# Attention and a gated MLP on one core: q loaded by rows of nine tokens, output stores in one DMA each, and new instruction lists

## The chip, the cores and the metric

The kernel runs on one core of a Trainium2 chip. The core has five engines, each with an instruction stream of its own: TensorE (PE) multiplies matrices, VectorE (DVE), ScalarE (ACT) and GpSimd (POOL) work on tiles, and SyncE (SP) here issues nearly all the transfers. Transfers between HBM and the core's SBUF run on 16 DMA engines, which all of them share. The engines meet through semaphores.

The metric is the device time of one execution in microseconds (us). Before the change the median of three runs is 245.94 us, from 245.34 to 246.67. A separate execution was recorded by the hardware profiler.

## The reference

There are 8 batches of 8 heads, 576 tokens of 64 values a head, and 32 packing queries `p` a head. Two softmax attentions follow each other, and then an MLP with a gated activation over all 4608 tokens:

```python
def _attn_ref(q, k, v, p):
    scale = 1.0 / np.sqrt(q.shape[-1])
    def sm_attn(qq, kk, vv):
        s = scale * np.matmul(qq, kk.transpose(0, 1, 3, 2))
        s = s - np.max(s, axis=-1, keepdims=True)
        a = np.exp(s)
        a = a / (np.sum(a, axis=-1, keepdims=True) + 1e-09)
        return np.matmul(a, vv)
    p_packed = sm_attn(p, k, v)
    return sm_attn(q, p_packed, p_packed)

def _moe_ref(x, w_in, w_out, beta):      # x: (4608, 512), heads side by side
    h = x @ w_in                         # (4608, 2048)
    g = h * (1.0 / (1.0 + np.exp(-beta * h)))
    return g @ w_out                     # (4608, 512)
```

All inputs and the output are float32.

## The kernel before

The work goes batch by batch, and several batches are under way at once. For each batch `b`:

- `plan_loads` loads k, q and v as float32 and casts them to bf16. For batches 0 and 1 (`PE_BATCHES = 2`) a partition takes nine tokens of a head in a row (`quarter`, L460: packets of 9 x 64 x 4 = 2304 bytes, two DMAs of 576 KB for each of k, q, v), the casts go to whichever engine the lists name, and TensorE transposes. For batches 2 to 7 there is one DMA of 1 MB (`main`, L444: a partition takes four tokens of a head, packets of 1 KB) for the first 512 tokens (`SM`), and two of 64 KB (`rest`, L452: 256-byte packets) for the last 64 (`SR`). GpSimd casts them in three pieces (`piece`, L476, and `tail`, L487). The float32 buffer of each of k, q, v exists once, so a load waits for the casts of the batch before; the bf16 buffer exists once too, so a cast waits for the last reader of the batch before.
- `transpose_dma` (L558) has k and q of batches 2 to 7 transposed by a DMA, issued on SP (task `("tr", b, x, 0)`).
- `plan_attention` computes scores `s1`, exponentials `e1`, sums `z1` and the packed values `pun`/`pp`; then the second attention: scores `s2` (L778, which needs the transposed q), `e2`, sums `z2`, and the normalised weights `A2`. Instead of forming the attention's output, it multiplies the packed values with `w_in` (`w`, giving `W`).
- `plan_mlp` has 16 blocks `h` (`W` times `A2`, activated by ACT into `g`) for the first 512 tokens, and `hr`/`gr` for the last 64. The product with `w_out` is made in plain form for batch 0 (tasks `o`), and for the others by seven products instead of eight (`plan_seven`, L1135: sums `S` on DVE, products `p`/`P` 1 to 7, results read by copies and additions `R11` to `R22+`).
- The result of a batch stands in two tiles `o_sb` of 512 KB, of which the pool holds two (`OUTS`). So `R11` of a batch waits until the first store of the batch before has landed, and `R22` until the second has; product 6 waits for `R11`, product 3 for `R22`. Each tile is stored by task `("store", n)`, where batch `b` has n = 2b and 2b + 1. For batches 0 and 1 a store is two DMAs of 256 KB in packets of 2 KB (L1028, L1189), for the others one DMA of 512 KB in packets of 4 KB (L1193). The last 64 tokens of two batches are stored together as `("store", b, 4)`.
- `plan_small` loads beta and p. The p rows of batches 0 and 1 come in two DMAs of 64 KB (`load_first`, L1283), those of all batches in one of 512 KB (`load_p`, L1287).

The order on each engine is fixed in advance: `SEQUENCE` (L62) lists every task by engine. `Planner.run` walks through these lists, and emits the instructions. It also puts small matmuls of ones (`keep_warm`, 128x128, written `o_ps<-ones` in the profile) into TensorE's stream where its estimate of the times leaves TensorE without work, up to 60 us. They compute nothing that is used, and once they are in the stream, TensorE runs them. The lists hold, for SP, the loads, the transposes, and the stores; SP waits at each for its conditions, and what is listed behind it waits too.

Of the kernel before, what the change touches and what calls it, by code (L numbers as in the profile page):

```python
# [8 lines left out]
B, H, S, D = 8, 8, 576, 64  # L9
# [12 lines left out]
NC = 4  # L22
# [24 lines left out]
PE_BATCHES = 2  # L47
HALVED = (0,)
def TILED(key):
# [14 lines left out]
        ("tr", 0, "k", 0), ("brow", 0), ("p0_tr", 0), ("bcol",), ("tr", 0, "k", 1), ("trr", 0, "k"), ("brow", 1),  # L64
        ("tr", 0, "q", 0), ("s1r", 0), ("s1", 0, 1), ("s1", 0, 0), ("tr", 0, "q", 1), ("p0_tr", 1), ("trr", 0, "q"),
        ("z1", 0), ("brow", 2), ("pun", 0, 0), ("pun", 0), ("tr", 1, "k", 0), ("s2", 0, 0), ("tr", 1, "k", 1),
        ("z2", 0, 0), ("s2", 0, 1), ("z2", 0, 1), ("w", 0, 0), ("tr", 1, "q", 0), ("trr", 1, "k"), ("z2", 0, 2),
        ("s1r", 1), ("s1", 1, 0), ("s1", 1, 1), ("w", 0, 1), ("h", 0, 1), ("h", 0, 0), ("h", 0, 3), ("h", 0, 7),
        ("tr", 1, "q", 1), ("h", 0, 2), ("h", 0, 6), ("z1", 1), ("o", 0, 2, 1), ("h", 0, 4), ("pun", 1, 0),
        ("pun", 1), ("brow", 3), ("h", 0, 5), ("o", 0, 3, 1), ("o", 0, 3, 3), ("o", 0, 2, 3), ("o", 0, 2, 5),  # L70
        ("s2", 1, 0), ("o", 0, 2, 7), ("o", 0, 3, 5), ("o", 0, 3, 7), ("z2", 1, 0), ("w", 0, 2), ("z2", 1, 1),
        ("o", 0, 0, 1), ("o", 0, 0, 3), ("w", 1, 0), ("o", 0, 1, 1), ("h", 0, 11), ("h", 0, 8), ("w", 0, 3),
        ("o", 0, 0, 5), ("o", 0, 0, 7), ("trr", 1, "q"), ("h", 0, 10), ("h", 0, 9), ("o", 0, 1, 3), ("w", 1, 1),
        ("h", 0, 14), ("h", 0, 13), ("w", 1, 2), ("h", 0, 15), ("h", 1, 6), ("w", 1, 3), ("h", 0, 12), ("o", 0, 1, 5),
        ("o", 0, 1, 7), ("h", 1, 1), ("h", 1, 11), ("p_tr", 0), ("h", 1, 4), ("h", 1, 8), ("p_tr", 1), ("o", 0, 0, 9),
        ("o", 0, 1, 9), ("h", 1, 2), ("o", 0, 0, 11), ("h", 1, 12), ("o", 0, 0, 13), ("h", 1, 9), ("o", 0, 0, 15),
        ("s2", 1, 1), ("h", 1, 10), ("h", 1, 0), ("o", 0, 1, 11), ("o", 0, 1, 13), ("o", 0, 1, 15), ("s1r", 2),
        ("s1", 2, 0), ("o", 0, 2, 9), ("h", 1, 5), ("h", 1, 14), ("s1", 2, 1), ("o", 0, 2, 11), ("o", 0, 3, 9),
        ("o", 0, 2, 13), ("o", 0, 2, 15), ("o", 0, 3, 11), ("z1", 2), ("o", 0, 3, 13), ("h", 1, 3), ("h", 1, 13),
        ("o", 0, 3, 15), ("h", 1, 15), ("h", 1, 7), ("p", 1, 1, 0), ("pun", 2, 0), ("z2", 1, 2), ("pun", 2),  # L80
        ("p", 1, 1, 1), ("p", 1, 1, 2), ("P", 1, 1), ("s2", 2, 0), ("s2", 2, 1), ("p", 1, 2, 0), ("hr", 0, 0),
        ("p", 1, 2, 1), ("p", 1, 2, 2), ("z2", 2, 0), ("P", 1, 2), ("hr", 0, 1), ("w", 2, 0), ("p", 1, 6, 0),
        ("p", 1, 6, 1), ("p", 1, 6, 2), ("P", 1, 6), ("p", 1, 5, 0), ("p", 1, 5, 1), ("p", 1, 5, 2), ("z2", 2, 1),
        ("hr", 1, 0), ("P", 1, 5), ("p", 1, 7, 0), ("s1r", 3), ("p", 1, 7, 1), ("s1", 3, 0), ("p", 1, 7, 2),
        ("s1", 3, 1), ("P", 1, 7), ("z2", 2, 2), ("p", 1, 3, 0), ("p", 1, 3, 1), ("p", 1, 3, 2), ("w", 2, 2),
        ("h", 2, 6), ("p", 1, 4, 0), ("p", 1, 4, 1), ("h", 2, 2), ("h", 2, 1), ("p", 1, 4, 2), ("z1", 3), ("h", 2, 8),
        ("h", 2, 9), ("P", 1, 4), ("pun", 3, 0), ("pun", 3), ("h", 2, 11), ("hr", 1, 1), ("o", 1, 4, 1), ("w", 3, 0),
        ("h", 2, 3), ("h", 2, 12), ("o", 1, 4, 3), ("P", 1, 3), ("h", 2, 13), ("h", 2, 7), ("o", 1, 4, 5),
        ("o", 1, 4, 7), ("h", 2, 0), ("h", 2, 15), ("o", 1, 4, 9), ("w", 3, 2), ("h", 2, 14), ("h", 2, 4),
        ("o", 1, 4, 11), ("o", 1, 4, 13), ("h", 2, 5), ("h", 2, 10), ("o", 1, 4, 15), ("p", 2, 1, 0), ("s2", 3, 0),  # L90
        ("s2", 3, 1), ("p", 2, 1, 1), ("p", 2, 1, 2), ("P", 2, 1), ("p", 2, 2, 0), ("p", 2, 2, 1), ("z2", 3, 0),
        ("p", 2, 2, 2), ("z2", 3, 1), ("p", 2, 6, 0), ("p", 2, 6, 1), ("p", 2, 6, 2), ("z2", 3, 2), ("P", 2, 6),
        ("P", 2, 2), ("s1r", 4), ("s1", 4, 1), ("s1", 4, 0), ("hr", 2, 0), ("p", 2, 7, 0), ("p", 2, 7, 1),
        ("p", 2, 5, 0), ("p", 2, 5, 1), ("p", 2, 7, 2), ("p", 2, 5, 2), ("P", 2, 5), ("h", 3, 8), ("h", 3, 12),
        ("z1", 4), ("pun", 4, 0), ("h", 3, 13), ("hr", 2, 1), ("pun", 4), ("P", 2, 7), ("p", 2, 3, 0), ("h", 3, 10),
        ("h", 3, 9), ("w", 4, 0), ("h", 3, 3), ("h", 3, 1), ("p", 2, 3, 1), ("h", 3, 2), ("p", 2, 3, 2), ("h", 3, 11),
        ("P", 2, 3), ("h", 3, 15), ("w", 4, 2), ("h", 3, 5), ("h", 3, 6), ("p", 2, 4, 0), ("p", 2, 4, 1), ("h", 3, 0),
        ("h", 3, 7), ("p", 2, 4, 2), ("P", 2, 4), ("h", 3, 4), ("h", 3, 14), ("s2", 4, 0), ("s2", 4, 1),
        ("p", 3, 1, 0), ("p", 3, 1, 1), ("p", 3, 1, 2), ("P", 3, 1), ("p", 3, 2, 0), ("p", 3, 2, 1), ("p", 3, 2, 2),
        ("z2", 4, 0), ("P", 3, 2), ("z2", 4, 1), ("p", 3, 6, 0), ("p", 3, 6, 1), ("p", 3, 6, 2), ("P", 3, 6),  # L100
        ("s1r", 5), ("s1", 5, 1), ("z2", 4, 2), ("s1", 5, 0), ("p", 3, 5, 0), ("p", 3, 5, 1), ("p", 3, 5, 2),
        ("p", 3, 7, 0), ("hr", 3, 0), ("P", 3, 5), ("p", 3, 7, 1), ("p", 3, 7, 2), ("h", 4, 6), ("z1", 5),
        ("h", 4, 13), ("P", 3, 7), ("hr", 3, 1), ("pun", 5, 0), ("h", 4, 1), ("p", 3, 3, 0), ("pun", 5), ("h", 4, 12),
        ("p", 3, 3, 1), ("h", 4, 14), ("p", 3, 3, 2), ("h", 4, 15), ("w", 5, 0), ("h", 4, 4), ("h", 4, 9),
        ("p", 3, 4, 0), ("p", 3, 4, 1), ("h", 4, 2), ("h", 4, 8), ("P", 3, 3), ("p", 3, 4, 2), ("h", 4, 0),
        ("h", 4, 7), ("P", 3, 4), ("w", 5, 2), ("h", 4, 3), ("h", 4, 10), ("o", 3, 4, 1), ("o", 3, 4, 3), ("h", 4, 5),
        ("h", 4, 11), ("o", 3, 4, 5), ("o", 3, 4, 7), ("o", 3, 4, 9), ("s2", 5, 0), ("s2", 5, 1), ("p", 4, 1, 0),
        ("o", 3, 4, 11), ("p", 4, 1, 1), ("z2", 5, 0), ("p", 4, 1, 2), ("P", 4, 1), ("z2", 5, 1), ("z2", 5, 2),
        ("o", 3, 4, 13), ("o", 3, 4, 15), ("p", 4, 6, 0), ("p", 4, 6, 1), ("hr", 4, 0), ("hr", 4, 1), ("p", 4, 2, 0),
        ("p", 4, 2, 1), ("p", 4, 2, 2), ("P", 4, 2), ("h", 5, 15), ("h", 5, 1), ("p", 4, 6, 2), ("P", 4, 6),  # L110
        ("h", 5, 3), ("h", 5, 10), ("s1r", 6), ("s1", 6, 0), ("p", 4, 5, 0), ("p", 4, 7, 0), ("p", 4, 5, 1),
        ("p", 4, 5, 2), ("s1", 6, 1), ("h", 5, 7), ("P", 4, 5), ("h", 5, 13), ("p", 4, 7, 1), ("p", 4, 7, 2),
        ("z1", 6), ("pun", 6, 0), ("P", 4, 7), ("p", 4, 3, 0), ("h", 5, 4), ("pun", 6), ("h", 5, 8), ("p", 4, 4, 0),
        ("p", 4, 3, 1), ("h", 5, 6), ("h", 5, 9), ("w", 6, 0), ("h", 5, 11), ("p", 4, 4, 1), ("h", 5, 0),
        ("p", 4, 3, 2), ("h", 5, 14), ("P", 4, 3), ("h", 5, 5), ("p", 4, 4, 2), ("h", 5, 2), ("P", 4, 4),
        ("h", 5, 12), ("s2", 6, 0), ("s2", 6, 1), ("hr", 5, 0), ("p", 5, 1, 0), ("p", 5, 1, 1), ("p", 5, 1, 2),
        ("P", 5, 1), ("p", 5, 2, 0), ("p", 5, 2, 1), ("z2", 6, 0), ("p", 5, 2, 2), ("z2", 6, 1), ("P", 5, 2),
        ("p", 5, 6, 0), ("p", 5, 6, 1), ("p", 5, 6, 2), ("P", 5, 6), ("s1r", 7), ("s1", 7, 1), ("p", 5, 5, 0),
        ("s1", 7, 0), ("z2", 6, 2), ("p", 5, 5, 1), ("p", 5, 5, 2), ("hr", 5, 1), ("P", 5, 5), ("p", 5, 7, 0),
        ("w", 6, 2), ("p", 5, 7, 1), ("p", 5, 7, 2), ("P", 5, 7), ("h", 6, 5), ("p", 5, 3, 0), ("p", 5, 3, 1),  # L120
        ("h", 6, 3), ("h", 6, 10), ("p", 5, 3, 2), ("p", 5, 4, 0), ("h", 6, 4), ("z1", 7), ("h", 6, 9), ("pun", 7, 0),
        ("pun", 7), ("h", 6, 0), ("P", 5, 3), ("h", 6, 2), ("p", 5, 4, 1), ("h", 6, 1), ("p", 5, 4, 2), ("h", 6, 15),
# [241 lines left out]
class Kernel:  # L364
# [65 lines left out]
    def plan_loads(self, b):  # L430
        nc = self.nc
        rank = 100 * b
        early = b < PE_BATCHES
        for xi, x in enumerate("kqv" if b == 0 else "kvq"):
            src = self.src[x]
            last = [] if b == 0 else [("cast", b - 1, x, i) for i in range(2)]
            lastr = [] if b == 0 else [("cast", b - 1, x, 2)]

            def opened(x=x, b=b):
# [1054 lines left out]
```

## Time and profile before

| | us |
|---|---|
| median of three runs | 245.94 |
| lowest and highest | 245.34, 246.67 |
| profiled execution: time | 247.44 |
| profiled execution: span, first to last instruction | 245.7 |
| TensorE busy in the span | 235.1 |
| ScalarE busy | 175.0 |
| VectorE busy | 157.6 |
| GpSimd busy | 54.8 |

The profiled execution is 1.5 us above the median. Its span leaves out 1.7 us around the first and the last instruction. Times in the profile count from the start of the span.

A busy share alone says little here: TensorE's stream contains the fillers, and matmuls overlap, with ends that are modelled. What TensorE needs for a task is read from the start of its first matmul to the start of the next task's. In lines of the timeline the columns are start, duration, engine and source line, operation, what is written and read, shape, count, and in brackets the idle time before it with what ended it. `SPq` is the issuing side of SyncE; the duration of a DMA there is the time that issuing it held SyncE, not its transfer.

The page also gives the mean granted TensorE clock, 0.993, and the DMA queue that SP uses: 67,504 packets and 53.75 MB, 80.3% of the 16 engines' time over the span.

### The profile page before, as it was taken

Reading aid. Unit: us, or ns where it says so; the run is one execution under the profiler, and the core shown is the slowest. Engines: PE = TensorE matmul, PEld = TensorE weight load, DVE = VectorE, ACT = ScalarE, POOL = GpSimd, SP = SyncE. Lnnn points to the kernel's source line nnn. Section 1 sums busy time; section 2 is a strip of 40 time slices with the busy share of each in tenths; the row PEclk is TensorE's granted clock in tenths of the full one; section 3 lists DMA queues with packets and bytes.
Section 4 is the critical chain, followed back from the end, with each engine's and each line's share of the span. In section 5 each row is a group of like instructions: output and inputs, shape, how many; then the busy total and the mean of one; then the engine's idle time right before and its main releaser. Section 6 shows DMA issues by size and latency. Waiting matters only on the chain.

```text
span 245.7 us, 6197 instructions
## 1 busy us (share of the span) xinstructions
PE 235.1 (96%) x2619; PEld 160.8 (65%) x2619; DVE 157.6 (64%) x259; ACT 175.0 (71%) x310; POOL 54.8 (22%) x73
## 2 busy tenths in 40 slices
PE   7999999999899998999899997899999999999993
PEld 7787743355578644884588554776687737668893
DVE  3858979996878668656875654544768157813821
ACT  4157879889779767876788679287787769868320
POOL 3211006424500726013503251060005100000000
PEclk9999999999999999999999999799999999999999
DMA  7999999999999998997899999969491640004124
GB/s 234 382 388 399 400 385 348 374 216 279 226 209 270 331 226 188 198 325 193 184 236 290 259 179 345 240 199 182 143 278 27 99 165 9 0 4 173 43 85 129
DMA packets 67699, 54.27 MB, mean 221 GB/s; under 512 B 39508, under 2 KB 59220, under 8 KB 67160
## 3 DMA queue, kind: packets, MB, share of 16 engines
q1 hardware_dynamic: 67504, 53.75, 80.3%
q8 instruction: 20, 0.33, 0.6%
q10 hardware_dynamic: 168, 0.14, 0.2%
q14 instruction: 7, 0.06, 0.1%
HBM read 37.36 MB, written 9.44 MB: 191 GB/s over the span
## 4 chain that ended last, share of the span: by engine, by line
PE 62%; DMA 19%; SPq 9%; DVE 3%; POOL 3%; ACT 2%; issue 1%; POOLq 0%; DVEq 0%
PE o_ps L395 34%; PE h_ps L395 15%; DMA k<-in_k_dram 8%; SPq L455 3%; DMA out_dram<-o_sb 3%; SPq L560 3%; DMA v<-in_v_dram 3%; DMA vr<-in_v_dram 2%; PE w_ps L395 2%; DMA qT<-q_bf 2%; PE s_ps L395 2%; PE hr_ps L395 2%; PE brow_ps L395 2%; DMA x<-in_moe_beta_dram 1%; SPq L1028 1%
## 5 line engine op out<-in xcount | busy, mean ns | idle before, releaser
L945 ACT ACTIVATE g_main<-h_ps 128x512 bf16<-128x512 f32 x128 | 72.0, 596 | 34.4 <-PE h_ps L395 34.1
L395 PEld LDWEIGHTS <-g_main 128*128 128x128 bf16 x624 | 59.5, 99 | 23.5 <-issue 2.4
L395 PE MATMUL h_ps<-A2T,W_bf 128*128 128x512 bf16 x256 | 69.7, 379 | 0.1
L395 PE MATMUL o_ps<-w_out_bf,g_main 128*128 128x256 bf16 (+1 forms) x400 | 61.8, 293 | 0.0
L910 DVE SCALAR_TENSOR_TENSOR W_bf<-w_ps,rz,beta_bc 128x512 bf16<-128x512 f32 x64 | 44.7, 744 | 16.6 <-PE w_ps L395 16.3
L395 PEld LDWEIGHTS <-W_bf 128*128 128x128 bf16 x512 | 33.1, 100 | 21.5 <-issue 6.3
L410 ACT ACT_TABLE_LOAD x24 | 30.8, 1283 | 1.1 <-PEq L1478 0.7
L395 PE MATMUL o_ps<-w_sum,g_main 128*128 128x256 bf16 x224 | 30.8, 273 | 0.0
L395 PE MATMUL o_ps<-w_sum,g_sum 128*128 128x256 bf16 x224 | 28.6, 273 | 2.2 <-DVE o_sb L1183 2.2
L1181 DVE TENSOR_TENSOR o_sb<-o_ps,o_sb 128x512 f32<-128x512 f32 x21 | 14.5, 689 | 21.4 <-PE o_ps L395 14.3
L395 PEld LDWEIGHTS <-g_sum 128*128 128x128 bf16 x224 | 21.3, 98 | 7.1 <-issue 2.5
L482 POOL CAST q_bf<-q 128x1024 bf16<-128x1024 f32 x12 | 13.0, 1093 | 57.2 <-DMA q<-in_q_dram 57.2
L1183 DVE COPY o_sb<-o_ps 128x512 f32<-128x512 f32 x16 | 11.0, 689 | 13.4 <-PE o_ps L395 9.3
L395 PE MATMUL o_ps<-ones 128*128 128x128 bf16 x219 | 17.5, 235 | 1.1 <-DVE ones L1246 1.1
L482 POOL CAST v_bf<-v 128x1024 bf16<-128x1024 f32 x12 | 12.4, 1047 | 23.9 <-DMA v<-in_v_dram 16.7
L482 POOL CAST k_bf<-k 128x1024 bf16<-128x1024 f32 x12 | 12.5, 1050 | 22.1 <-DMA kT<-k_bf 9.4
L395 PEld LDWEIGHTS <-ones 128*128 128x128 bf16 x219 | 14.9, 107 | 3.3 <-issue 1.6
L395 PE MATMUL o_ps<-w_out_bf,g_rem 128*128 128x512 bf16 (+1 forms) x80 | 16.5, 336 | 0.0
L965 ACT ACTIVATE g_rem<-hr_ps 128x512 bf16<-128x512 f32 x16 | 9.3, 596 | 7.6 <-PE hr_ps L395 7.6
L1151 DVE TENSOR_TENSOR g_sum<-g_main 128x2048 bf16<-128x2048 bf16 x7 | 9.0, 1279 | 6.9 <-ACT g_main L945 6.9
L810 ACT ACTIVATE E2T<-s_ps,rz 128x512 bf16<-128x512 f32 x16 | 10.6, 685 | 3.7 <-PE s_ps L395 2.0
L395 PEld LDWEIGHTS <-pp 64*32 64x32 bf16 x368 | 3.9, 89 | 12.9 <-issue 7.6
(111 smaller groups left out, 264.5 us busy)
## 6 DMA issues: line engine op xcount, KB each, us to landing
k<-in_k_dram SPq DMA_DIRECT2D x6, 1024.0 KB, 11.0
q<-in_q_dram SPq DMA_DIRECT2D x6, 1024.0 KB, 7.7
v<-in_v_dram SPq DMA_DIRECT2D x6, 1024.0 KB, 8.1
out_dram<-o_sb SPq DMA_DIRECT2D x10, 512.0 KB, 3.1
w_in<-in_moe_w_in_dram SPq DMA_DIRECT2D x4, 1024.0 KB, 10.3
w_out<-in_moe_w_out_dram SPq DMA_DIRECT2D x4, 1024.0 KB, 11.8
out_dram<-o_sb SPq DMA_DIRECT2D x12, 256.0 KB, 3.6
k<-in_k_dram SPq DMA_DIRECT2D x4, 576.0 KB, 6.4
```

The lines of the kernel that those rows point to most:

```text
L395: return self.nc.tensor.matmul(out, lhsT, rhs, start=start, stop=stop, tile_position=pos, skip_group_check=True)
L410: self.nc.scalar.preload_act_table_set(SETS[mode])
L455: nc.sync.dma_start(t[64 * g : 64 * g + 64, :].rearrange("p (h d) -> p h d", h=4), src[b, 4 * g : 4 * g + 4, SM:S, :].rearrange("h p d -> ...
L482: self.copy[engine](o[:, 0:2048].rearrange("p (t h d) -> p h t d", t=4, h=8)[:, h], t[:, 0:2048].rearrange("p (h t d) -> p h t d", h=8, t= ...
L560: nc.sync.dma_start_transpose(t[:], st[b, x][:])
L810: nc.scalar.activation(st[b, "E2"][:, i, 0:SM], st[b, "s2", i][:], AF.Exp, scale=st[b, "rz1"][:, 2 + i : 3 + i])
L910: nc.vector.scalar_tensor_tensor(st[b, "W"][:, r, cols].rearrange("q (f p) -> q f p", f=4), st[b, "w", m][:].rearrange("q (p f) -> q f p", ...
L945: nc.scalar.activation(st[b, "g"][:, ft, :], st[b, "h", ft][:], AF.Silu)
L965: nc.scalar.activation(st[b // 2, "gr"][:, 8 * half : 8 * half + 8, o : o + 64], st[b, "hr", half][:].rearrange("p (f n) -> p f n", f=8), ...
L1151: nc.vector.tensor_tensor(o, x, y, op)
L1181: nc.vector.tensor_tensor(o, x, o, ALU.add)
L1183: self.copy[engine](o, x)
```

## The change

Four things are changed together.

1. **q of batches 2 to 6** (`BY_ROWS`) is loaded with nine tokens of a head in each partition, as in the early batches: four DMAs of 288 KB with packets of 2304 bytes (`pairs`). GpSimd casts it in two halves, each of four instructions, which also order the tokens in such a way that a partition of the output tile holds two neighbouring rows of the output. The scores `s2` read the transposed q by this order. q of batch 7, and all k and v, stay as they were, except that the last 64 tokens now stand in the same float32 buffer as the others, so that the next batch's load waits for all three casts.
2. **Stores**: with the tokens in this order the two tiles of batches 0 to 6 are each stored by one DMA with packets of 4 KB (`self.rows`). For batches 0 and 1 this replaces two DMAs of 2 KB packets; their q is transposed in another order for it.
3. **p**: the rows of batches 0 and 1 come in one DMA of 128 KB, and are cast, transposed (four matmuls) and placed together; the other load has only batches 2 to 7.
4. **The lists** of all five engines are replaced. Tasks move along their list, and some change their engine.

```diff
+BY_ROWS = range(2, 7)
...
+            def pairs(i, x=x, b=b, src=src, opened=opened):
+                t = opened() if i == 0 else self.t[b, x, "32"]
+                for e in range(2):
+                    nc.sync.dma_start(
+                        t[:].rearrange("p (i e f) -> p i e f", i=2, e=2)[:, i, e],
+                        src[b].rearrange("(a i e) (s t) d -> i e a s (t d)", e=2, i=2, t=TS)[i, e],
+                    )
...
+                if rows:
+                    for e in range(2):
+                        o = self.t[b, x][:, h].rearrange("p (t e d) -> p e t d", t=TS, e=2)[:, e]
+                        n = self.t[b, x, "32"][:, h].rearrange("p (e t d) -> p e t d", t=TS, e=2)[:, e]
+                        self.copy[engine](
+                            o[:, 0:8].rearrange("p (r m e) d -> p r e m d", r=2, m=2),
+                            n[:, 0:8].rearrange("p (r e m) d -> p r e m d", r=2, m=2),
+                        )
+                        self.copy[engine](o[:, 8], n[:, 8])
+                    return
...
+                    if b in BY_ROWS:
+                        q = q[h, TS * (c % 2) : TS * (c % 2) + TS, g : g + 64]
+                        q = q[:, 8] if rest else q[:, 0:8]
...
-                if b < PE_BATCHES:
-                    rows = self.out[S * b : S * b + S, :].rearrange("(s t) n -> s t n", t=TS)
-                    for e in range(2):
-                        nc.sync.dma_start(rows[:, 2 * t - 2 + e : 2 * t + 1 + e : 2], o[64 * e : 64 * e + 64])
+                if b < PE_BATCHES or b in BY_ROWS:
+                    nc.sync.dma_start(self.rows(b, t // 2), o[:])
                     return
...
+    def rows(self, b, i):
+        rows = self.out[S * b : S * b + S, :].rearrange("(s t) n -> s t n", t=TS)[:, 4 * i : 4 * i + 4]
+        return rows.rearrange("s (e m) n -> e s (m n)", e=2)
...
-        def load_first(b):
-            self.p0[b] = t = self.sm.tile([128, 2, D], f32, tag="E2T", name="p0")
-            nc.sync.dma_start(t[:], self.p[b].rearrange("(e x) s d -> (x s) e d", e=2))
+        def load_first():
+            self.p0 = t = self.sm.tile([128, 4 * D], f32, tag="E2T", name="p0")
+            nc.sync.dma_start(t[:], self.p[0:PE_BATCHES].rearrange("b h (x t) d -> (b h x) (t d)", t=4))
```

The list of SP from the first q by rows to the last load of batch 6, before and after:

```diff
-        ("ld", 2, "q", 0), ("tr", 2, "k", 0), ("ld", 2, "q", 2), ("ld", 2, "v", 0), ("ld", 2, "v", 2),
-        ("ld", 3, "k", 0), ("ld", 3, "k", 2), ("tr", 2, "q", 0), ("store", 0), ("store", 1), ("tr", 3, "k", 0),
-        ("ld", 3, "v", 0), ("ld", 3, "v", 2), ("ld", 3, "q", 0), ("ld", 4, "k", 0), ("ld", 3, "q", 2),
-        ("ld", 4, "v", 0), ("ld", 4, "k", 2), ("ld", 4, "v", 2), ("tr", 3, "q", 0), ("store", 2), ("tr", 4, "k", 0),
-        ("store", 3), ("ld", 4, "q", 0), ("ld", 5, "k", 0), ("ld", 5, "k", 2), ("ld", 4, "q", 2), ("ld", 5, "v", 0),
-        ("tr", 4, "q", 0), ("store", 4), ("tr", 5, "k", 0), ("store", 5), ("ld", 5, "q", 0), ("ld", 5, "q", 2),
-        ("ld", 5, "v", 2), ("ld", 6, "k", 0), ("ld", 6, "k", 2), ("ld", 6, "v", 0), ("ld", 6, "v", 2),
-        ("tr", 5, "q", 0), ("ld", 6, "q", 0), ("store", 1, 4), ("store", 7), ("store", 6), ("ld", 7, "k", 0),
+        ("ld", 2, "q", 0), ("ld", 2, "q", 1), ("tr", 2, "k", 0), ("ld", 2, "v", 0), ("ld", 2, "v", 2),
+        ("ld", 3, "k", 0), ("ld", 3, "k", 2), ("tr", 2, "q", 0), ("store", 0), ("ld", 3, "v", 0), ("tr", 3, "k", 0),
+        ("store", 1), ("ld", 3, "v", 2), ("ld", 3, "q", 0), ("ld", 3, "q", 1), ("ld", 4, "k", 0), ("ld", 4, "v", 0),
+        ("ld", 4, "v", 2), ("ld", 4, "k", 2), ("ld", 4, "q", 0), ("tr", 3, "q", 0), ("store", 2), ("tr", 4, "k", 0),
+        ("ld", 4, "q", 1), ("store", 3), ("ld", 5, "v", 0), ("store", 1, 4), ("ld", 5, "k", 0), ("ld", 5, "q", 0),
+        ("ld", 5, "k", 2), ("tr", 4, "q", 0), ("ld", 5, "q", 1), ("ld", 6, "k", 0), ("store", 4), ("tr", 5, "k", 0),
+        ("store", 5), ("ld", 5, "v", 2), ("tr", 5, "q", 0), ("ld", 6, "q", 0), ("ld", 6, "v", 0), ("ld", 6, "k", 2),
+        ("ld", 6, "v", 2), ("ld", 6, "q", 1), ("store", 7), ("store", 6), ("ld", 7, "k", 0),
```

At the start of the lists, the casts, transposes and copies of the first two batches are dealt out among ACT, DVE and POOL in another way. For example, ACT now casts the second half of k of batch 1 before the exponentials `e2` of batch 0, and DVE casts a half of the second `w_in` block between `A2` 0 of batch 0 and `W` 0 of batch 0.

## Prediction

> **What bounds the kernel now.** I read the page first (busy shares and the 40 slices), then TensorE's timeline, the list of waits, the busy times by stage, and SyncE's queue.
>
> ```profile
> span 245.7 us, 6197 instructions
> ...
> PE 235.1 (96%) x2619; PEld 160.8 (65%) x2619; DVE 157.6 (64%) x259; ACT 175.0 (71%) x310; POOL 54.8 (22%) x73
> ...
> PEclk9999999999999999999999999799999999999999
> DMA  7999999999999998997899999969491640004124
> ```
>
> TensorE is issuing nearly all the time, and the DMA engines are full for the first 60% of the span. So there are two questions: what of TensorE's time is no work, and which transfer it waits for. The timeline of TensorE answers the first (start, duration, shape and count; in brackets the idle time before it and what ended it):
>
> ```profile
> 17.58 1.17 PE L395 MATMUL o_ps<-ones 128*128 128x128 bf16 x18
> ...
> 23.41 1.61 PE L395 MATMUL o_ps<-ones 128*128 128x128 bf16 x26
> ...
> 67.90 0.41 PE L395 MATMUL s_ps<-qT,pp 64*32 64x512 bf16 x8 [0.99 <-DMA qT<-q_bf]
> ...
> 97.12 0.41 PE L395 MATMUL s_ps<-qT,pp 64*32 64x512 bf16 x8 [0.71 <-DMA qT<-q_bf]
> ...
> 121.74 0.41 PE L395 MATMUL s_ps<-qT,pp 64*32 64x512 bf16 x8 [1.22 <-DMA qT<-q_bf]
> ...
> 154.24 1.03 PE L395 MATMUL o_ps<-w_sum,g_sum 128*128 128x256 bf16 x8 [2.23 <-DVE o_sb L1183]
> ...
> 156.76 2.80 PE L395 MATMUL o_ps<-w_out_bf,g_main 128*128 128x256 bf16 x16
> ...
> 177.18 2.79 PE L395 MATMUL o_ps<-w_out_bf,g_main 128*128 128x256 bf16 x24
> ```
>
> Ends are modelled, so I count from start to start. The `ones` matmuls are fillers, 0.056 us each (eighteen from 17.58 to 18.67, less 0.09 for a change of tile shape). From the first `h` at 27.11 on, real work follows back to back, except in four places: before `s2` of batches 2, 3 and 4, which wait for the transposed q, and at 152 us. Start to start these cost 1.06, 0.78 and 1.29, and 2.3 us. After the last one TensorE is slow: 16 matmuls of 256 columns take 2.64 us (to 159.40), where 24 take 2.62 at 177.18, so these 16 lose 0.9, and the `hr` before them 0.7. The stage view has the granted clock of that stretch (PE, PEld, DVE, ACT, POOL busy, clock, DMA share, GB/s):
>
> ```profile
> 150.00:160.00 10.00, 7.77 (x74) 5.93 (x72) 4.03 (x6) 5.26 (x9) 1.04 (x1) 0.83 1.05 280
> ```
>
> What held 152 us is in the waits (us, times, longest) and in SyncE's queue:
>
> ```profile
> DVE o_sb L1183 <- DMA out_dram<-o_sb: 4.1, 2, 3.6
> ```
>
> ```profile
> 140.12 3.40 SPq L560 DMA_TRANSPOSE qT<-q_bf  x1
> 143.57 0.58 SPq L447 DMA_DIRECT2D q<-in_q_dram  x1
> 144.20 1.22 SPq L1038 DMA_DIRECT2D out_dram<-o_rest  x2
> 145.52 1.34 SPq L1193 DMA_DIRECT2D out_dram<-o_sb  x2
> 146.96 0.45 SPq L447 DMA_DIRECT2D k<-in_k_dram  x1
> 147.51 10.00 SPq L560 DMA_TRANSPOSE kT<-k_bf  x1
> ```
>
> The stores of batch 3 stand behind a 1 MB load, so the copy that reuses their buffer waits. A transpose holds SyncE until what was queued before it has landed: this k transpose for 10.00 us, until 157.51; the loaded k landed at 157.43. After 160 us the DMA share falls below 1, and TensorE has no gaps over 0.3 us. The avoidable time is 1.06 + 0.78 + 1.29 + 2.3 + 1.6 = 7.0 us, plus what part of the 219 fillers (12.4 us) earlier data would remove.
>
> **The change, part by part.**
>
> *The start.* The changed program has 189 fillers, 30 fewer: 30 x 0.056 = -1.7 us. Two more p transposes cost +0.1; 16 transposes of 96 columns in place of 128 give -0.2. That is -1.8 if data comes in time. The DMA share is 1.04 to 1.08 from 4 us on, so I walked the landings: the one p load is 128 packets of 1 KB in place of 512 of 256 B, which by the packet times in the trace (46 and 18 ns, 16 engines) is 0.37 for 0.58 us, so the loads of batch 1 come about 0.4 us earlier. In the new order `s2` of batch 0 can start near 16.3 (18.67 before). The gain shrinks at ACT, where the cast of k (1.15 us) now stands ahead of the first exp, and at VectorE, where a weight cast of the second `w_in` stands ahead of `W` 0: landing 22.0, cast 0.7, reciprocal 0.25, then `W` 0.75, q cast 0.75, `W` 0.75, `A2` 0.68, so first `h` at 26.5, not 27.1. With the 12 fewer fillers after it (0.7): **-1.2**, bounds 0 and -1.8.
>
> *q by rows, batches 2 to 6.* Before, 1024 packets of 1 KB and 512 of 256 B a batch; after, 512 of 2304 B. The nearest rows are the early q and v loads (576 KB in the same packets), which land 1.5 us apart; I take 1.6 each for later crowding, 3.2 a batch. A 1 MB load takes 3.5 (landings between 76.7 and 92.6 are 3.1 to 4.7 us apart) and a pair of 64 KB 0.6: 4.1. So -0.9 a batch, bounds 0 and -1.1. [...]
> GpSimd's casts become 2 x (512 + 64) elements for each half. Rows of 1.04 us for 1024 and 0.40 for 256 give 0.62 and 0.24: 1.7 a half, 3.4 a batch for 2.5. GpSimd is 22% busy and the transposes wait for the queue anyway: nothing; uncovered it would be +0.9 a batch. `s2` reads 64 columns at a time for 128, the same 512: nothing, bounds 0 and +0.1 a batch.
>
> *Stores of batches 0 and 1 as one DMA of 4 KB packets.* Before, two stores took 5.1 us of the queue (67.6 to 72.7), 2.5 each; a 512 KB store in 4 KB packets and the k transpose behind it took 4.6 us (121.7 to 126.3), less 3.0 for a transpose (64.6 to 67.6): 1.6. I take 1.8, so 4 x -0.7 = -2.8 us, bounds 0 and -3.6.
>
> *The queue's new order*, where gain and loss lie. I walk it from the k transpose of batch 2 (landing 54.5, now 53.7: the two p loads and q are 0.8 shorter). It runs at 1.06 of the sum of these prices: from there to 126.3 the old order sums to 67.8 and took 71.8. Due times are TensorE's durations by kind (`h` or `o` 0.43 a pair, `p` 0.44, `hr` 0.47, `w` 0.56, `s1` 0.23, `s2` 0.37) summed in the new order from the first `h` at 26.5, with the new waits as they come.
> - q of batch 2: v, k, transpose, 11.4 x 1.06 = 12.1, lands 65.8 (67.6 before); `s2` is due about 66.6. Gap gone.
> - Store 1 now stands behind the v load of batch 3 and a k transpose: 1.8 + 3.5 + 3.2 + 1.8, x 1.06, lands 76.7. The copy of quarter 22 of batch 1 needs its buffer, and product 3 behind it is due at 76.2: 76.7 + 0.7 copy + 0.3 gives 77.7, **+1.4**, bounds 0 and +2.5 (store as dear as before, 0.7, and queue at 1.10). Behind that copy VectorE holds `A2` of batch 2, not due for 1.5 us.
> - q of batches 3 and 4: land near 94.5 and 117, due near 95.9 and 118. Both gaps gone.
> - k of batch 5: its transpose now has q of batch 5 (3.2), k of batch 6 (3.5) and a small store (0.7) ahead that stood behind it before. Old landing 126.3, less 0.8, less 0.9 x 2 q batches and 0.9 on q of batch 4, less 2.8, plus 7.4: 127.4. `s1` of batch 5 is due near 125.4: **+2.0**, bounds 0 and +6. Store 4 stands just ahead, lands near 124, and holds quarter 11 of batch 3, due 121.9, by 1 us of the same 2.
> - Stores 7 and 6: q of batch 5 lands 133, five loads behind it end near 142, store 7 lands near 144 and 6 near 147; needed at 149. The 2.3 us gap and the slow clock behind it go: -3.9.
> - From 150 on the transposes land 2 us and more ahead of their use. The tail of 3.7 us after TensorE's last matmul has the same stores: nothing.
>
> Sum: -1.2 - 7.0 + 1.4 + 2.0 + 0.6 for smaller waits like the three of 0.2 to 0.3 us in the trace of before = **-4.2 us**. That is made on the profiled execution (span 245.7, time 247.4, so span 241.5, time 243.2). It lies 1.5 above the runs' median, 245.94, from which -4.2 gives **241.7 us**. Half a per cent, 1.2 us, is about what a measurement of this kernel can tell from no change.
>
> **The rivals.**
> - *The new waits don't come* (queue at 1.00 of the prices): -1.8 - 7.0 + 0.3 = -8.5, 237.4 us. For: the early stage's 1.5 us spacing. Against: 71.8 for 67.8. Chance 0.12.
> - *The waits only move:* both new waits at the upper middle of their bounds, +2.2 and +4.2 with 1.6 of slow clock, as after the 2.2 us idle: -1.2 - 7.0 + 8.0 = -0.2, 245.7 us (with 0.6 of small waits, 246.3). For: the stretch from 54.5 to 76.7 ran at 1.10. Chance 0.16.
> - *Slower: k of batch 5 decides.* Loads of batches 5 and 6 now run ahead of its transpose. If the queue runs at 1.15, it lands at 53.7 + 69.7 x 1.15 = 133.9 (69.7 is the new sum), 8.5 us late, plus 1.6 of clock: -1.2 - 7.0 + 1.4 + 10.1 = +3.3, 249.2 us. It decides from a landing past 130.5. For: 72 us of full queue lie ahead of it and nothing can overtake. Against: no stretch above 1.10. The same comes if rows and 4 KB packets save nothing (the change not doing what it says): +0.9 x 3 + 2.8 = 5.5 later. Chance 0.14.
> - My forecast, 0.58, with its own range 239.5 to 244.0.
>
> **The numbers.** Faster: 0.58 x 0.98, 0.12, and a quarter of the second rival's 0.16: 0.73. Same: the rest of that case and a little of the forecast: 0.13. Slower: 0.14. The range leaves out half of the first rival and most of the third: 238.5 to 246.5.
>
> **What would show it.** Right: `s2` of batches 2 to 4 without idle time on the q transposes; no gap near 152 and a clock of 1.00 there; 576 KB q loads at 3.2 us of queue a batch; gaps of 1 to 2 us at 76 (behind a store) and at 125 (behind kT). Wrong: first `h` not before 27.1; kT of batch 5 landing past 130; a stall over 2 us with the clock below 0.9 behind it; or gaps on VectorE or ACT work, which the trace of before doesn't have after 27 us and the new lists could bring.

## The result and the profile after

| | before | after |
|---|---|---|
| median, us | 245.97 | 440.44 |
| lowest and highest, us | 245.34, 246.67 | 440.14, 441.58 |
| ratio, 95% interval | | 1.791 (1.786 to 1.797) |
| span of the profiled execution, us | 245.7 | 438.3 |
| mean granted TensorE clock | 0.993 | 0.800 |

Here and below, ratios and their intervals leave out executions that took over 1.5% longer than the fastest of the same kernel, and medians count all.

The forecast was 241.7 us, in a range of 238.5 to 246.5. The kernel became 79% slower. The page of the changed kernel, first the busy times, then three rows of the 40 slices, then the chain of work that ended last:

```profile
span 438.3 us, 6166 instructions
...
PE 267.9 (61%) x2591; PEld 173.6 (40%) x2591; DVE 155.2 (35%) x251; ACT 179.5 (41%) x316; POOL 63.8 (15%) x100
...
PE   8999920937592033908170469702398459979386
...
PEclk9999975788698557976875588955889598969869
DMA  8999694973145993424949395214899390110113
...
DMA 37%; SPq 33%; PE 23%; DVE 2%; issue 2%; ACT 1%; POOL 1%; ACTq 0%; DVEq 0%; POOLq 0%
```

VectorE and ScalarE are busy for about as long as before (155.2 and 179.5 us against 157.6 and 175.0), and GpSimd for 9.0 us more (63.8 against 54.8): their work does not explain 194 us. TensorE stands idle in whole slices, the DMA row is low at the same time, and the chain of waits is made of transfers (37%) and of SyncE standing at its issues (33%). So the machine waits for transfers while the transfer engines look idle. The waits name them (us, times, longest):

```profile
POOL q_bf L509 <- DMA q<-in_q_dram: 102.7, 16, 19.3
...
DVE o_sb L1215 <- DMA out_dram<-o_sb: 61.9, 5, 23.1
ACT o_sb L1215 <- DMA out_dram<-o_sb: 61.8, 6, 22.8
```

These are the two transfers that the change rewrote: q by rows, and the stores of rows. VectorE's copies into a reused output tile waited 4.1 us for stores before. The first place is at 40 us, in SyncE's queue and in the stages (in the second view: PE, PEld, DVE, ACT, POOL busy, clock, DMA share, GB/s):

```profile
40.64 17.73 SPq L470 DMA_DIRECT2D q<-in_q_dram  x4
58.48 15.22 SPq L585 DMA_TRANSPOSE kT<-k_bf  x1
```

```profile
52.00:58.00 6.00, 5.91 (x35) 2.39 (x32) 5.91 (x11) 5.46 (x10) 0.85 (x2) 1.00 0.13 50
58.00:64.00 6.00, 0.00 (x0) 0.00 (x0) 1.74 (x2) 0.71 (x3) 0.79 (x2) 0.77 0.13 50
```

From 52 to 64 us only q loads of batch 2 move. The DMA share is 0.13, which is 2/16, and the rate 50 GB/s, for 359 to 400 between 10 and 50 us of the kernel before. So, by the share, two engines of 16 carry them and 14 stand still. In the trace's packet records, exactly two packets are under way for some 151 us of the changed kernel, for 3 or 4 us of the kernel before. The median packet is as long as before (95 ns for 2304 bytes in both; 160 ns before and 159 after for 4096). By that, a load of 288 KB takes 128 x 95 / 2 = 6.1 us, and a store of 512 KB 128 x 159 / 2 = 10.2 us; from first to last packet the trace has 5.9 to 7.7 us and 10.0 to 11.9. There are 20 such loads and 14 such stores: 122 + 143 us on two engines.

What the two transfers share is the shape of their HBM side: `[2, 64, 576]` for a load and `[2, 64, 1024]` for a store. The outermost count is 2. Every large load and store of the kernel before has 64 or more there.

That the count of 2 holds the DMA share at 2/16 is a guess up to here; the experiments test it.

Behind the waits, the clock: where TensorE has nothing to do it falls to 0.77 (58 to 64 us) and to 0.50 (64 to 70 us). It does not cause the idle time: in 52 to 58 us the clock is 1.00 and the share already 0.13.

### The profile page after: what moved, and what is told of

Its sections match the earlier page's. It is cut to its first block, busy times and chain, and to the rows that moved or that the text cites. A ratio compares the mean times of both kernels' runs of the same rounds, so it can differ in the third digit from the quotient of the medians.

```text
span 438.3 us, 6166 instructions
## 1 busy us (share of the span) xinstructions
PE 267.9 (61%) x2591; PEld 173.6 (40%) x2591; DVE 155.2 (35%) x251; ACT 179.5 (41%) x316; POOL 63.8 (15%) x100
## 4 chain that ended last, share of the span: by engine, by line
DMA 37%; SPq 33%; PE 23%; DVE 2%; issue 2%; ACT 1%; POOL 1%; ACTq 0%; DVEq 0%; POOLq 0%
DMA out_dram<-o_sb 23%; SPq L585 16%; PE o_ps L394 12%; SPq L470 9%; PE h_ps L394 7%; DMA kT<-k_bf 5%; SPq L447 3%; DMA v<-in_v_dram 3%; SPq L455 3%; DMA qT<-q_bf 2%; DMA k<-in_k_dram 2%; SPq L1219 2%; DMA w_in<-in_moe_w_in_dram 1%; PE w_ps L394 1%; PE s_ps L394 1%
## 5 line engine op out<-in xcount | busy, mean ns | idle before, releaser
L394 PE MATMUL o_ps<-w_sum,g_sum 128*128 128x256 bf16 x224 | 42.3, 353 | 74.0 <-ACT o_sb L1215 49.4
L394 PEld LDWEIGHTS <-g_main 128*128 128x128 bf16 x624 | 64.0, 105 | 52.2 <-issue 28.0
L394 PE MATMUL o_ps<-w_out_bf,g_main 128*128 128x256 bf16 (+1 forms) x400 | 70.4, 320 | 21.1 <-DVE o_sb L1215 20.0
L394 PE MATMUL h_ps<-A2T,W_bf 128*128 128x512 bf16 x256 | 76.2, 401 | 5.4 <-DVE A2T L881 5.4
L394 PEld LDWEIGHTS <-g_sum 128*128 128x128 bf16 x224 | 27.0, 125 | 86.9 <-issue 78.6
L1215 ACT COPY o_sb<-o_ps 128x512 f32<-128x512 f32 x13 | 7.6, 586 | 66.4 <-DMA out_dram<-o_sb 61.8
L509 POOL CAST q_bf<-q 128x512 bf16<-128x512 f32 x20 | 13.2, 662 | 115.8 <-DMA q<-in_q_dram 102.7
L394 PE MATMUL s_ps<-qT,pp 64*32 64x512 bf16 x56 | 3.7, 449 | 34.9 <-DMA qT<-q_bf 34.9
L394 PEld LDWEIGHTS <-kT 128*128 128x128 bf16 (+1 forms) x180 | 8.2, 117 | 27.1 <-DMA kT<-k_bf 25.5
L394 PE MATMUL s1r_ps<-pT,kT 128*128 128x128 bf16 (+1 forms) x20 | 2.8, 259 | 24.6 <-DMA kT<-k_bf 24.6
```

The costliest lines, as they stand in the source:

```text
L394: return self.nc.tensor.matmul(out, lhsT, rhs, start=start, stop=stop, tile_position=pos, skip_group_check=True)
L509: self.copy[engine](o[:, 0:8].rearrange("p (r m e) d -> p r e m d", r=2, m=2), n[:, 0:8].rearrange("p (r e m) d -> p r e m d", r=2, m=2),)
L1215: self.copy[engine](o, x)
```

## The experiments

Each was executed at least once, with a profile; where an interval is given, there are 6 or 12 executions, beside 11 to 23 of the kernel before. Theory: a transfer runs on as many engines as its outermost count allows. The rivals: the new lists or GpSimd's casts of q by rows are at fault, or only one of the two transfers is.

**Loads on 16 engines, stores as changed.**

```diff
-                for e in range(2):
+                for a in range(2):
                     nc.sync.dma_start(
-                        t[:].rearrange("p (i e f) -> p i e f", i=2, e=2)[:, i, e],
-                        src[b].rearrange("(a i e) (s t) d -> i e a s (t d)", e=2, i=2, t=TS)[i, e],
+                        t[64 * a : 64 * a + 64].rearrange("p (i e f) -> p i e f", i=2, e=2)[:, i],
+                        src[b].rearrange("(a i e) (s t) d -> i a s e (t d)", e=2, i=2, t=TS)[i, a],
                     )
```

> The changed kernel, with the four DMAs of a batch's q cut by partition halves, so that each HBM side has 64 as its outermost count in place of 2; bytes, packets of 2304 bytes and the order stay. Theory (a DMA runs on as many of the 16 engines as its outermost count allows, so the q loads and the stores of rows each run on 2): the loads spread out and only the 14 stores stay on two engines: 150 us of other work per engine + 15 of q + 143 of stores = about 310 to 330 us, bounds 300 to 345; the stretches with q loads alone show a DMA share near 1 instead of 0.13. Rival 1 (the lists or GpSimd's casts of q by rows are the cause): about 440, as the changed kernel. Rival 2 (only the loads matter, the stores lie beside other work): about 242 to 250.

**Stores on 16 engines, loads as changed.**

```diff
-                nc.sync.dma_start(self.rows(b, row), st[b, "ob", row][:])
+                for e in range(2):
+                    nc.sync.dma_start(self.rows(b, row)[e], st[b, "ob", row][64 * e : 64 * e + 64])
```

> The changed kernel, with each store of rows given as two DMAs of 256 KB whose outermost count is 64; packets of 4 KB and the order stay, the q loads stay as changed. Theory: only the 20 q loads of batches 2 to 6 stay on two engines: 150 us of other work per engine + 122 of q + 18 of stores = about 290 to 335 us, with the DMA share of 0.13 remaining in the stretches of q loads and the waits of the copies for their output buffers gone. Rival 1 (lists or casts): about 440. Rival 2 (only the stores matter): about 242 to 250.

**Both edits.**

> Both of these edits: the changed lists, casts, token order, p load and packet sizes, with all transfers on 16 engines. Theory: the whole loss is gone, and what my forecast priced is left: 238 to 246 us, with 241.7 the likeliest; gaps of 1 to 2 us on TensorE near 76 us behind a store and near 125 us behind the transposed k of batch 5, none near 152 us. Rival 1 (lists or casts): above 300 still. Rival 3 (rows and 4 KB packets save nothing in the queue either): 247 to 252.

In the stretches with q loads (the columns as above), the first run has a DMA share near 1, the second still 0.13:

```profile
50.00:54.00 4.00, 1.71 (x13) 0.75 (x11) 1.87 (x4) 1.87 (x4) 0.01 (x1) 1.00 1.04 224
```

```profile
54.00:58.00 4.00, 3.76 (x24) 1.42 (x23) 3.92 (x6) 3.83 (x6) 0.85 (x2) 1.00 0.13 50
```

Measured: 346.35 us with the loads mended, 346.5 with the stores mended, 257.86 with both (257.49 to 258.82; ratio to before 1.059, 1.054 to 1.065). Each edit alone takes off 94 us, both together 183: the losses nearly add. So does the time with exactly two packets under way: some 151 us as changed, then 69, 70 and 2. Rivals 1 and 2 are out. My sums for the single edits were too low, by 16 and 11 us at their upper ends; they left out the slower clock (0.879 and 0.871) and something that the third run shows by itself: with all transfers on 16 engines the kernel is still 5.9% slower than before. That lies outside the theory's 238 to 246 us, and outside rival 3's 247 to 252.

**The other direction: the kernel before, with four of its stores put on two engines.**

```diff
-                    for e in range(2):
-                        nc.sync.dma_start(rows[:, 2 * t - 2 + e : 2 * t + 1 + e : 2], o[64 * e : 64 * e + 64])
+                    nc.sync.dma_start(rows[:, 2 * t - 2 : 2 * t + 2].rearrange("s (e m) n -> e s (m n)", e=2), o[:])
```

(and the same for batch 1.)

> The kernel before, with the two tiles of batches 0 and 1 each stored by one DMA with an outermost count of 2 and packets of 4 KB, in place of two DMAs with an outermost count of 64 and packets of 2 KB; pairs of output rows of these two batches are exchanged by it, everything else stays. Theory: four stores of 10.2 us on two engines, which the loads behind them and the copies wait for: 20 to 35 us slower than before, 266 to 281. Rival 1 (lists or casts): as before, 244 to 248. If a two-engine store runs beside other transfers at no cost: 244 to 250 too.

**The same with the two outer dimensions in the other order**, `"s (e m) n -> s e (m n)"`:

> The kernel before, with the two tiles of batches 0 and 1 each stored by one DMA in packets of 4 KB, as in the run with outermost 2, but with the HBM side ordered [64, 2, 1024]; bytes, packets and the number of DMAs are those of that run (272.7 us), only the order of the two outer dimensions differs. Output rows of these two batches are exchanged. Theory (the outermost count sets the engines): the loss of 27 us is gone, and each store costs 1.3 to 1.8 us of the queue for 2.5 before: 242 to 246 us, up to 3 below before. Rival (one DMA of 512 KB, or packets of 4 KB beside loads, is what costs): 265 and more.

Measured: 272.66 us and 241.95 us (ratio to before 0.989, 0.985 to 0.993). Bytes, packets and the number of DMAs are the same in both; only the order of two dimensions differs, and it is worth 31 us in four stores. In the run of 272.66 us, the stage view has nothing but such stores at work for a while:

```profile
68.00:70.00 2.00, 1.77 (x41) 1.48 (x42) 1.09 (x1) 1.30 (x3) 0.02 (x1) 1.00 0.13 53
70.00:72.00 2.00, 2.00 (x43) 1.48 (x40) 0.00 (x0) 1.55 (x5) 0.00 (x0) 1.00 0.13 53
```

**Counts of 4 and 8**, in the kernel before, for batches 2, 4, 6 and 3, 5:

```diff
+            if b < 7:
+                y = 4 if b % 2 == 0 else 8
+                nc.sync.dma_start(rows.rearrange("(x y) t n -> y x (t n)", y=y), st[b, "ob", row][:])
+                return
```

> The kernel before, with the stores of batches 2 to 6 (one DMA of 128 packets of 4 KB each) given with an outermost count of 4 for batches 2, 4, 6 and of 8 for batches 3, 5 in place of 128; output rows of these batches are exchanged. Theory: the DMA share while nothing but such a store moves is 4/16 = 0.25 and 8/16 = 0.50, a store takes 32 x 0.159 = 5.1 us and 16 x 0.159 = 2.5 us on its engines, and the whole 248 to 262 us. Rival (a count of 2 is a special slow case, or any two-dimensional side is slow): shares of 0.13 or 1.0 for both, and 280 or 246 us.

Measured: 280.51 us. From 227 to 230 us only a store of count 8 moves, from 251 to 255 one of count 4:

```profile
227.00:230.00 3.00, 3.00 (x33) 1.56 (x32) 0.88 (x1) 2.34 (x4) 0.00 (x0) 1.00 0.49 91
...
251.00:255.00 4.00, 4.00 (x49) 3.54 (x48) 2.45 (x2) 3.05 (x5) 0.00 (x0) 1.00 0.22 50
```

The shares are 8/16 and nearly 4/16, as the theory has it; the rival's 0.13 or 1.0 does not occur. The time isn't as the theory has it: 280.51 us lies outside its 248 to 262, the stores of count 4 took 6.7 to 10.2 us each and not 5.1, those of count 8 took 3.7 to 4.8 and not 2.5 (first to last packet). In the two windows shown a packet takes 348 and 289 ns on average, for 159. The shares are shown; why the packets also went more slowly here is open.

**What is left at 257.9 us.** In that kernel each of the rewritten DMAs covers 64 partitions. The packets of 2304 bytes take 158 to 174 ns where q comes by rows (medians by batch), for 95 ns in the first 20 us; those of 4096 bytes take 253 to 328 ns in ten of the 14 stores, and 159 in the other four. All 16 engines are busy: from 82.2 to 86 us, with q loads alone, the DMA share is 0.99, but the rate 233 GB/s. So I kept the DMAs over 128 partitions and changed which token a partition holds, so that the outermost count is 64 all the same:

```diff
-                        src[b].rearrange("(a i e) (s t) d -> i e a s (t d)", e=2, i=2, t=TS)[i, e],
+                        src[b].rearrange("(a i e) (s t) d -> i e s a (t d)", e=2, i=2, t=TS)[i, e],
...
+                    j = slice(c // 2, 128, 2)
...
-                        q = q[h, TS * (c % 2) : TS * (c % 2) + TS, g : g + 64]
+                        q = q[h, TS * (c % 2) : TS * (c % 2) + TS, j]
...
+            if b < PE_BATCHES or b in BY_ROWS:
+                o = o.rearrange("p (g s e) -> p g e s", g=4, e=2)
+                x = x.rearrange("p (g e s) -> p g e s", g=4, e=2)
...
-        return rows.rearrange("s (e m) n -> e s (m n)", e=2)
+        return rows.rearrange("s (e m) n -> s e (m n)", e=2)
```

> The changed kernel, with its transfers over all 128 partitions and 16 engines at once: a partition of q holds token s of head a at 2s + a (not 64a + s), a partition of an output tile rows of s and e at 2s + e (not 64e + s), so that the HBM sides run [64, 2, 576] and [64, 2, 1024]; the scores read every second column of the transposed q, and the exponentials write every second column. The order of the lists stays. In the kernel with halves of 64 partitions the packets of 2304 B took 160 to 180 ns where q is loaded by rows and 95 ns in the first 20 us, those of 4096 B up to 330 for 159. Theory A (the halves are what is left of the loss: a DMA over 64 partitions moves at half the rate): packets back at 95 and 159 ns, q of a batch 3.0 to 3.5 us of the queue, transposed k of batch 5 before 130 us, and 239 to 246 us in all, with 241.7 the likeliest, as my forecast has it. Theory B (the new lists themselves are late, as my third rival has it: k of batch 5 decides): packets as in A, but the k lands past 132 us, TensorE still has a gap of 4 us and more near 130 us, and the time is 248 to 257. If the strided reads and writes cost TensorE or ScalarE time: matmuls s_ps<-qT,pp longer than 0.41 us for 8, or exponentials over 0.68 us each.

Measured: 246.11 us (243.03 to 248.99), ratio 1.004 (1.000 to 1.009). The packets are back at 93 to 101 ns for q and 156 to 200 for the stores (medians), with q loads alone (78.6 to 79.4 us) the rate is 392 GB/s at a share of 1.01, and 12 us are gone: theory A for the transfers. But it isn't 241.7, and the gap that theory B named is there too. TensorE's timeline has one large gap (start, duration, shape, count, idle time before it):

```profile
68.38 0.42 PE L394 MATMUL s_ps<-qT,pp 64*32 64x512 bf16 x8 [0.59 <-DMA qT<-q_bf]
78.55 1.47 PE L394 MATMUL o_ps<-w_out_bf,g_main 128*128 128x256 bf16 x12 [0.43 <-DVE o_sb L1218]
...
128.97 1.01 PE L394 MATMUL o_ps<-w_sum,g_sum 128*128 128x256 bf16 x4 [4.30 <-ACT o_sb L1218]
```

```profile
120.00:130.00 10.00, 5.70 (x56) 4.50 (x56) 3.85 (x4) 5.28 (x10) 2.60 (x5) 0.90 1.02 253
130.00:140.00 10.00, 10.00 (x114) 8.03 (x113) 3.86 (x9) 6.86 (x14) 2.92 (x6) 0.76 0.92 238
```

and SyncE's queue says what lay ahead of it:

```profile
117.80 0.48 SPq L447 DMA_DIRECT2D k<-in_k_dram  x1
118.38 0.62 SPq L1222 DMA_DIRECT2D out_dram<-o_sb  x1
119.10 8.75 SPq L585 DMA_TRANSPOSE kT<-k_bf  x1
```

Product 6 of batch 3 waits for a copy, the copy for store 4, and store 4 stands behind the 1 MB load of k of batch 6: the store landed at 127.96. The transposed k of batch 5, behind both, landed at 129.96. From 129.0 to 134.8 us the tasks, start to start, take 2.8 us more than their kinds do elsewhere; the clock is 0.50 there. This profiled execution took 248.6 us with a mean clock of 0.986, above the median, so the gap is shown at its dearest: two of the twelve executions kept a clock of 1.00 and took 243.0 and 243.3 us, and how long they waited here isn't known.

**That load behind the store and the transpose:**

```diff
-("ld", 6, "k", 0), ("store", 4), ("tr", 5, "k", 0),
+("store", 4), ("tr", 5, "k", 0), ("ld", 6, "k", 0),
```

> The kernel with all its transfers over 128 partitions and 16 engines (246.1 us), with one step of SP's list moved: the 1 MB load of k of batch 6 goes behind store 4 and the transpose of k of batch 5, not ahead of them. Theory (the one gap left, 4.3 us at 129 us with a clock of 0.76 behind it, comes from store 4 and the k of batch 5 standing behind that load): store 4 lands before 124.5 instead of at 127.96, the gap falls under 1 us, the clock stays at 1.00 in 130 to 140, and the time falls by 3 to 6 us: 240 to 243. Rival (the gap only moves to the k of batch 6 or to store 5): 244 to 248.

Measured: 243.02 us, ratio 0.990 (0.986 to 0.994). Store 4 lands at 123.81, the k at 125.91, the gap is gone, and one of 1.06 us at 133 us (behind a cast of v) is the largest left. The clock holds in the profiled execution (two of the twelve still have 0.986 and 0.993):

```profile
130.00:140.00 10.00, 8.83 (x113) 5.75 (x121) 6.27 (x12) 5.93 (x11) 2.92 (x6) 1.00 1.16 291
```

**The parts alone, in the lists of before.** Stores of batches 0 and 1 over 128 partitions in one DMA, output in place:

```diff
+                t = n if x == "k" else n // 4 * 4 + n % 2 * 2 + n // 2 % 2
...
+            if b < PE_BATCHES:
+                o = o.rearrange("p (g s e) -> p g e s", g=4, e=2)
+                x = x.rearrange("p (g e s) -> p g e s", g=4, e=2)
...
-                for e in range(2):
-                    nc.sync.dma_start(rows[:, 4 * row + e : 4 * row + 3 + e : 2], st[b, "ob", row][64 * e : 64 * e + 64])
+                nc.sync.dma_start(self.rows(b, row), st[b, "ob", row][:])
```

> The kernel before, with nothing changed but the stores of batches 0 and 1: one DMA of 512 KB each in packets of 4 KB over 128 partitions, the output rows in their right places (q of these batches transposed in the changed kernel's order, and the exponentials of the second attention written to every second column). Theory: as the run with exchanged rows, 241 to 243.5 us, ratio 0.985 to 0.995. Rival (the strided write costs ScalarE time that TensorE waits for): 244 to 247.

Measured: 241.95 us, ratio 0.988 (0.983 to 0.992). q by rows alone, with the loads, casts and scores of the 246.1 us version; in the lists of before, its second load follows the first directly, and the loads and casts of the last 64 tokens fall away. For example:

```diff
-("ld", 4, "q", 0), ("ld", 5, "k", 0), ("ld", 5, "k", 2), ("ld", 4, "q", 2),
+("ld", 4, "q", 0), ("ld", 4, "q", 1), ("ld", 5, "k", 0), ("ld", 5, "k", 2),
```

> The kernel before with q of batches 2 to 6 by rows alone, over 128 partitions and 16 engines (second half directly behind the first), in the lists of before; the stores of batches 0 and 1 are two DMAs each, as before, and those of batches 2 to 6 one DMA of 4 KB packets, as before, with the rows of the new token order. Theory (my forecast's term: 0.9 us of queue a batch saved, the waits for the transposed q of batches 2 to 4 shortened): 1 to 3 us faster, 242 to 244.5. Rival (a load by rows saves nothing that TensorE waits for; what the version with all transfers gained over before came from the stores of batches 0 and 1): 244.5 to 247.

Measured: 244.58 us, ratio 0.999 (0.995 to 1.002). Both:

> The lists of the kernel before, with the changed transfers over 128 partitions and 16 engines: q of batches 2 to 6 by rows (its second half loaded directly behind the first, in place of the two small loads further behind), the stores of batches 0 to 6 as one DMA in packets of 4 KB; p, the casts of the start and the order of the lists as before. Theory (the transfers save 0.9 us of queue a batch of q and 1 us a store, the new lists give part of it back at store 4): 239 to 243 us, with the waits for the transposed q of batches 2 to 4 shortened. Rival (the new order is what brings the gain, the transfers bring none): 244 to 247.

Measured: 244.26 us, ratio 0.992 (0.989 to 0.996). So the gain over before comes from the four stores; q by rows gives none by itself. The profile of the run with q alone says why. The waits for the transposed q go, except one of 0.65 us at 119.5, and another wait takes their place

```profile
119.50 0.42 PE L396 MATMUL s_ps<-qT,pp 64*32 64x512 bf16 x8 [0.65 <-DMA qT<-q_bf]
...
158.61 0.28 PE L396 MATMUL s1r_ps<-pT,kT 128*128 128x128 bf16 x2 [2.94 <-DMA kT<-k_bf]
```

and likewise in the run with both, 3.30 us at 158.21. The clock in 150 to 160 us is 0.86 there (an execution of 246.6 us), and 1.00 in the run with q alone. In the run with both, the 1 MB load of k of batch 7 is issued at 144.88, and the transpose of k of batch 6 behind it holds SyncE for 8.03 us. So, last, the transpose ahead of that load, in the run with both:

```diff
-("ld", 7, "k", 0), ("tr", 6, "k", 0),
+("tr", 6, "k", 0), ("ld", 7, "k", 0),
```

> The version with the lists of before and all changed transfers on 16 engines (244.3 us, ratio 0.992), with the transpose of k of batch 6 moved ahead of the 1 MB load of k of batch 7 in SP's list. In that version the waits for the transposed q are gone, but TensorE idles 3.3 us at 158 us for the transposed k of batch 6, with a clock of 0.86 behind it. Theory (queue order alone makes that wait): the transpose waits for store 6, which landed at 149.96, lands near 153, the gap falls under 1 us, the clock stays at 1.00 in 150 to 160, and the time falls by 2 to 5 us, to 239 to 242, ratio 0.975 to 0.985 to before, the best of all versions. Rival (the wait only moves on to batch 7 or the stores): 243 to 246.

Measured: 240.99 us (240.47 to 241.80), ratio 0.986 (0.982 to 0.991). The transposed k lands at 152.21, the wait for it is gone, the largest gap left is 1.35 us at 149.6 (behind a copy), and the stage has its clock:

```profile
150.00:160.00 10.00, 9.89 (x116) 7.97 (x117) 5.59 (x8) 7.14 (x14) 2.06 (x3) 1.00 0.96 265
```

That the wait went is shown; the step in time is less sure, since the interval overlaps that of the run without the move (0.989 to 0.996). This version and the one with the stores alone beat both kernels, by 1.4% and 1.2% of the kernel before; the two can't be told apart.

## Why the prediction was wrong, point by point

- **The step that failed: the prices of the new transfers.** "q by rows, batches 2 to 6" took 1.6 us for 576 KB from "the early q and v loads", and so -0.9 a batch with bounds 0 and -1.1; "Stores of batches 0 and 1" took 1.8 us, bounds 0 and -3.6; the stores of batches 2 to 6 got no new price, since they remained one DMA of 4 KB packets. All three looked at bytes and packet sizes. Those rows belong to transfers over 16 engines (a DMA share of 1.04 to 1.06 between 10 and 50 us of the kernel before), and the new ones run on two (0.13): 12.2 us for 576 KB and 10.2 us for a store by the packets; from first to last packet the changed kernel's trace has 12.0 us for the first 576 KB of q of batch 2 and 10.0 to 11.9 us a store. The bounds shut out a loss, though nothing in the trace of before had such a shape; the diff shows the 2, in `i e a s` and in `e s`.
- With 64 and 128 partitions set right, **the prices themselves were about right**: loads of 288 KB land 0.7 to 0.8 us apart (51.52, 52.27, 52.98; 136.50, 137.22; one pair 1.1), 2.9 to 3.2 a batch for 3.2 forecast; in the kernel before with one-DMA stores, store 1 lands 1.4 us (exchanged rows) and 1.8 us (rows in place) behind store 0, for 1.8.
- **The four gaps, -7.0.** In the version of 246.1 us the waits for q of batches 3 and 4 and the gap near 152 are gone, with a clock of 1.00 in 150 to 160. Before `s2` of batch 2, 0.59 stayed; I had it gone: the transposed k of batch 2 landed at 56.09, not at 53.7, and all behind it was later. And 1.6 of the 7.0 was the slow clock of one execution, with a mean clock of 0.993: of the 79 executions of the kernel before that ran beside the experiments, 77 have 0.996 or more, so this part was mostly not there to be gained.
- **Store 1, +1.4:** it landed at 77.72 (76.7 forecast) and cost 0.43. Bounds held.
- **k of batch 5, +2.0:** the right place and the right neighbour, mis-sized. It landed at 129.96 for 127.4, and store 4 "near 124" at 127.96, so the store and not the k held TensorE, for 4.3 us and 2.8 of slow clock: 7.1 in that execution, for 2.0. The queue ran at 1.09 of the prices up to there ((129.96 - 53.7) / 69.7), not at 1.06, and store 4, which the same 1 MB load held up, was put at 1 us of these 2. With that load behind both of them, they land at 123.81 and 125.91.
- **The start, -1.2:** first `h` at 26.95 in the version of 246.1 us, 27.42 in that of 243.0 and 27.44 in the changed kernel itself, for 26.5 forecast and 27.11 before; with 12 fewer fillers after it (0.7), about -0.9 to -0.4.
- **The chance given to slower** rested on a queue at 1.15 of the prices. With 64-partition transfers it ran at 1.22 ((138.65 - 53.7) / 69.7, by the landing of k of batch 5), past the third rival, and the time was 257.9 us, not 249.2. For 440 us there was no case at all.

## What to carry to other kernels

Price a changed DMA by the order of its dimensions first and by its bytes second: read the outermost count of the HBM side in the diff. Here a count of 2 gave a DMA share of 0.13 with packets of 2304 and of 4096 bytes, 4 and 8 gave 0.22 and 0.49 with 4096, and 64 gave 1.01 with 2304. A rewrite that gives longer packets can give them to fewer engines: the stores of batches 0 and 1 went from 2 KB packets to 4 KB ones at that share of 0.13, and with these four stores alone the kernel before took 272.66 us. And when transfers become faster, look again at which load stands ahead of which store or transpose in the queue: two such pairs stood in TensorE's way here, and moving them took the ratio from 1.004 to 0.990 and, less surely, from 0.992 to 0.986.

## What the runs showed of the hardware that was not expected

- Most DMAs of 64 partitions on 16 engines moved at little more than half the rate: 2304-byte packets took 158 to 174 ns for 93 to 101 over 128 partitions, 12 us of the kernel's time. The stores of batch 1 in the kernel before have 64 partitions too, and their 2 KB packets take 146 ns (median), for 87 between 31 and 38 us; those of batch 0, whose four DMAs are issued within 3 us, take 84. That this is what one DMA a store gains its 1.2% from is likely, and not shown. Why 64 partitions are slower is open.
- How long TensorE idles did not alone decide its clock. Idle times of 2.23 us (before), 3.30 (the changed transfers in the lists of before), 4.30 (the version of 246.1 us) and 5.13 (that of 257.9 us) were followed by a mean clock of 0.52 to 0.72 over the next 6 us; idle times of 2.59 us (257.9 us version, at 80.6 us) and 2.94 us (q by rows alone) by 1.00. What else decides is open.
- An exponential that writes every second bf16 column takes 0.83 us for 0.69 contiguous (128x512). It cost no time that shows: the kernel before with one-DMA stores took 241.95 us with four such exponentials and with none.
